# Attention and two feed-forward layers on one core: where the softmax probabilities of the later head pairs are divided by their sums

## The chip, the core and the metric

The kernel runs on one core of one Trainium2 chip. A core has five engines that run side by side, each with its own instruction queue worked off in order: TensorE (PE in the profile, its weight loads PEld), VectorE (DVE), ScalarE (ACT), GpSimd (POOL) and SyncE (SP), which here only issues DMAs. The metric is the device time of one execution in microseconds, the median of several runs.

## What is computed

```python
def _attn_ref(q, k, v, g_q, g_k):
    q_n, k_n = (rmsnorm(q, g_q), rmsnorm(k, g_k))
    scores = scale * np.matmul(q_n, k_n.transpose(0, 1, 3, 2))
    scores = scores - np.max(scores, axis=-1, keepdims=True)
    attn = np.exp(scores)
    attn = attn / (np.sum(attn, axis=-1, keepdims=True) + 1e-09)
    return np.matmul(attn, v)

x = attn_out.transpose(0, 2, 1, 3).reshape(B * S, H * D)
h = x @ w_in;  g = s * np.maximum(h, 0) ** 2 + b;  x = g @ w_out
h = x @ w2_in; g = h * np.cos(h);                  out = g @ w2_out
```

There are 4 batches of 12 heads, 448 positions and 64 values a head. The two feed-forward layers see 1792 rows of 768 values and are 2048 wide. Inputs of q, k, v are float32, the weights float64.

## The kernel before

**The work.** Two heads make a pair, so there are 24 pairs, six to a batch. A pair has four chunks of query rows: three of 128 rows, each for both heads, and a last one in which the 64 remaining rows of both heads share one tile. One step of the attention works on one chunk: `scores` multiplies q by k on TensorE (tile `sc`, in PSUM), VectorE finds the row maximum (`top`), and ScalarE takes the exponential into `pr` and adds up each row into `sums`. Two steps later `turn` transposes `pr` on TensorE in four pieces (tile `tp`) and VectorE and ScalarE copy the turned pieces to `pT`. When all four chunks of a pair are turned, `mix` multiplies `pT` by v on TensorE (tile `av`).

**The division.** The probabilities are not divided one by one. `reciprocals` lets GpSimd add 1e-9 to the seven columns of `sums`, VectorE takes reciprocals, and GpSimd spreads them over 64 columns each into `rb`. `spread` transposes `rb` on TensorE (four 128x128 pieces, tile `rt`, lines 354 to 361), so that the reciprocal of every query stands above its column, and ScalarE copies `rt` to `xf`. `finish` multiplies `av` by `xf` on VectorE. Then `keep` either splits the result into a high and a low half for the feed-forward layers (batches 0 and 1: `xha` on ScalarE, `xla` on GpSimd) or sends it to DRAM to be fetched back later (batches 2 and 3).

**The order of the work.** The first nine pairs (`ALONE = 9`) run nearly by themselves. From the tenth on, attention steps are woven between units of the first feed-forward layer: an "in" unit (tile `ph`, 18 matmuls of 448 columns, then ScalarE, GpSimd and VectorE make `gh` and `gl`) and an "out" unit (tile `po`, 6 matmuls, then VectorE adds it to `acc`, or ScalarE copies it there the first time). Every step returns a cost, a number that only paces the weaving. Weights are float64 and are taken apart by bit operations on VectorE (`c`, `t`), then split into `wh` on ScalarE and `wl` on GpSimd. The order in which each engine gets its instructions is settled when the program is built; at run time each engine takes them strictly in that order.

**Buffers that the steps speak of.** In the woven part `ph` and `po` take turns in two PSUM buffers (tag `mo`), so a unit can start when the unit two before it has been emptied. The score tiles, and from the tenth pair on also `pt`, `rt` and `av`, take turns in a ring of four PSUM buffers (tag `sc`, function `four`); a transposed chunk has two (`tp`). `pr` has six buffers in SBUF. `line("PE", ...)` chains all attention work on TensorE in one fixed order.

Of the kernel before, what the change touches and what calls it, by code (L numbers as in the profile page):

```python
# [10 lines left out]
F32 = mybir.dt.float32  # L11
# [4 lines left out]
ALU = mybir.AluOpType  # L16
# [17 lines left out]
def body(ctx, tc, q, k, v, g_q, g_k, w1_in, w1_out, s_in, b_in, w2_in, w2_out, out):  # L34
# [4 lines left out]
    P = 128  # L39
# [69 lines left out]
    def split(src, layer, b, eng=nc.gpsimd):  # L109
        done = xs.setdefault((layer, b), [])  # L110
        hi, lo = (z[:, b % 2 * S:(b % 2 + 1) * S] for z in home(layer, b)[len(done)])
        nc.scalar.copy(hi, src)  # L112
        eng.tensor_tensor(lo, src, hi.bitcast(F32), ALU.subtract)
        done.append(True)

# [18 lines left out]
    def attention(keep):  # L134
# [151 lines left out]
        def scores(s):  # L286
# [36 lines left out]
            exps.append(e)  # L323

# [9 lines left out]
        def turn(s):  # L334
            i, c = divmod(s, NCH)
            b, hp = pairs[i]
            if c == 0:
                for j in range(2):
                    st[i]["pT", j] = att.tile([CP, NCH, S], F32, tag=f"pT{j}", name=f"pT_{b}_{hp}_{j}")
            for z in range(2 if c < NW else 1):  # L340
# [5 lines left out]
                for j in ((z,) if c < NW else (0, 1)):  # L346
                    at, part = (slice(c * P, (c + 1) * P), src) if c < NW else (slice(CUT, S), src[:, :, j * HALF:(j + 1) * HALF])
                    dst = st[i]["pT", j][:, :, at]
                    if j:
                        line("DVE", nc.vector.tensor_copy(dst, part))  # L350
                    else:
                        line("ACT", nc.scalar.copy(dst, part))

        def spread(i):
            b, hp = pairs[i]
            rt = bank(i, (i, "r"), f"rt_{b}_{hp}")
# [4 lines left out]
            line("ACT", emptied((i, "r"), nc.scalar.copy(x[D:, CUT:], rt[D:, S:])))  # L361

        def mix(i, part):
# [4 lines left out]
            for kc in part:  # L368
                for j in range(2):
                    mm.append(nc.tensor.matmul(st[i]["pa"][j * D:(j + 1) * D, :], st[i]["v"][:, j, kc, :], st[i]["pT", j][:, kc, :], start=(kc == 0), stop=(kc == NCH - 1)))  # L370
# [4 lines left out]
        def finish(i):  # L375
            b, hp = pairs[i]
            x = st[i]["x"]
            line("DVE", emptied((i, "a"), nc.vector.tensor_tensor(x, st[i]["pa"], x, ALU.mult)))
            st[i].clear()
            if i < ALONE - 1:  # L380
                held.append((b, hp, x))
            else:
                keep(b, hp, x)
                finished["pairs"] += 1
# [30 lines left out]
        for s in range(n + 5):  # L415
# [10 lines left out]
            if r == 3 and old is not None and not alone:  # L426
                spread(old)
                mix(old, range(NCH))
                finish(old)
                cost += 3.86  # L430
# [11 lines left out]
            if r == 0:  # L442
                if 0 <= i - 2 < ALONE:
                    finish(i - 2)
                emit(reciprocals, i - 1)
# [381 lines left out]
```

## Time and profile before

| what | value |
|---|---|
| median of 3 runs | 1264.2 us (1260.06 to 1722.74) |
| profiled execution, its own time | 1266.07 us |
| its span in the profile | 1263.9 us |
| PE busy | 1235.9 us |
| DVE busy | 834.9 us |
| ACT busy | 745.0 us |
| POOL busy | 604.6 us |
| mean granted TensorE clock | 0.997 |

The span is the time from the first to the last recorded instruction; some 2 us of the execution's own time lie around it. Busy is the time in which an engine had at least one instruction in work. Matmuls overlap, so a matmul's own duration is longer than the distance from its start to the next one's; in this kernel the distances tell what a matmul costs.

### The profile page before, as it was taken

To read this page: it belongs to the slowest core of one execution; us is meant where nothing else is said; L and a number is where in the kernel's file an instruction comes from. 1 tells how busy PE (TensorE), PEld (TensorE's weight loads), DVE (VectorE), ACT (ScalarE), POOL (GpSimd) and SP (SyncE) were. 2 spreads that over 40 slices of the span, in tenths; PEclk is the share of its full clock that TensorE was granted. 3 is DMA by queue.
4 is the path that set the end of the run, shared out by engine and by line. 5 is a ranking of instruction groups with operands and counts; after the bars stand their busy time and mean duration, and the time that the engine had idled before them with its cause. 6 is when DMAs were issued, how large, how long until landed. Compare 5 with 4: busy or idle time off the path is not lost.

```text
span 1263.9 us, 18827 instructions
## 1 busy us (share of the span) xinstructions
PE 1235.9 (98%) x6629; PEld 1046.1 (83%) x6629; DVE 834.9 (66%) x1447; ACT 745.0 (59%) x1665; POOL 604.6 (48%) x724
## 2 busy tenths in 40 slices
PE   7999999999999999999999999999999999999998
PEld 5454677777786877889999999899999999999998
DVE  6777868868767674843444447765867766666755
ACT  5777888866665664435332225698665757566741
POOL 4666646555644425724332323555453535354531
PEclk9999999999999999999999999999999999999999
DMA  4233345534433333442221112121202111111105
GB/s 125 77 109 88 110 118 147 152 112 134 129 104 99 118 120 121 149 143 92 80 65 56 57 44 76 38 75 64 75 28 73 51 50 51 51 51 51 52 12 175
DMA packets 86734, 111.33 MB, mean 88 GB/s; under 512 B 11760, under 2 KB 76784, under 8 KB 86640
## 3 DMA queue, kind: packets, MB, share of 16 engines
q1 hardware_dynamic: 86320, 109.90, 28.5%
q8 instruction: 52, 0.85, 0.3%
q14 instruction: 42, 0.34, 0.1%
q10 hardware_dynamic: 320, 0.23, 0.1%
HBM read 86.51 MB, written 23.59 MB: 87 GB/s over the span
## 4 chain that ended last, share of the span: by engine, by line
PE 52%; ACT 2%; DVE 2%; POOL 1%; DMA 1%; issue 1%; POOLq 0%; SPq 0%; DVEq 0%; ACTq 0%
PE ph L547 25%; PE po L632 18%; PE po L606 9%; DMA raw<-in_moe_w_in_dram 1%; POOL wl L475 0%; DVE t L516 0%; ACT xha L112 0%; POOL gt L576 0%; ACT t L510 0%; DVE acc L614 0%; DVE gt L572 0%; ACT gh L577 0%; DVE t L517 0%; DVE c L515 0%; ACT wh L472 0%
## 5 line engine op out<-in xcount | busy, mean ns | idle before, releaser
L578 POOL TENSOR_TENSOR gl<-gt,gh 128x448 fp32r<-128x448 f32 (+2 forms) x128 | 152.0, 1194 | 165.0 <-ACT gh L577 164.9
L547 PE MATMUL ph<-xha,wh 128*128 128x448 f32 (+2 forms) x576 | 212.2, 370 | 1.3 <-DVE acc L614 0.8
L547 PE MATMUL ph<-xha,wl 128*128 128x448 f32 (+2 forms) x576 | 211.2, 367 | 0.0
L547 PE MATMUL ph<-xla,wh 128*128 128x448 f32 (+2 forms) x576 | 211.0, 367 | 0.0
L475 POOL TENSOR_TENSOR wl<-t,wh 128x384 fp32r<-128x384 f32 x128 | 139.9, 1109 | 97.5 <-ACT wh L472 93.0
L472 ACT CAST wh<-t 128x384 fp32r<-128x384 f32 x200 | 95.6, 512 | 114.8 <-PE po L606 48.7
L614 DVE TENSOR_TENSOR acc<-po,acc 128x448 f32<-128x448 f32 x168 | 102.5, 617 | 75.6 <-PE po L606 75.4
L632 PE MATMUL po<-wh,gh 128*128 128x384 f32 x448 | 151.5, 339 | 0.0
L632 PE MATMUL po<-wl,gh 128*128 128x384 f32 x448 | 150.1, 335 | 0.4 <-POOL wl L475 0.4
L632 PE MATMUL po<-wh,gl 128*128 128x384 f32 x448 | 150.2, 335 | 0.0
L606 PE MATMUL po<-gh,wh 128*128 128x448 f32 x384 | 144.8, 380 | 1.5 <-DVE acc L614 1.4
L640 DVE TENSOR_TENSOR acc<-po,acc 128x384 f32<-128x384 f32 x196 | 105.1, 550 | 60.0 <-PE po L632 59.9
L606 PE MATMUL po<-gh,wl 128*128 128x448 f32 x384 | 140.8, 367 | 0.0
L606 PE MATMUL po<-gl,wh 128*128 128x448 f32 x384 | 140.7, 367 | 0.0
L576 POOL TENSOR_TENSOR gt<-hs,gt 128x512 f32<-128x512 f32 x64 | 76.3, 1200 | 118.7 <-ACT gt L575 114.8
L321 ACT ACTIVATE pr<-sc,top 128x448 f32<-128x448 f32 x161 | 101.8, 638 | 43.6 <-DVE top L312 43.3
L516 DVE SCALAR_TENSOR_TENSOR t<-c,t 128x384 uint32<-128x384 uint32 x128 | 94.9, 745 | 42.2 <-ACT t L510 39.1
L561 POOL TENSOR_TENSOR r<-r 128x448 f32<-128x448 f32 x64 | 63.1, 986 | 120.6 <-ACT r L559 106.0
L547 PEld LDWEIGHTS ph<-xha,wh 128*128 128x128 f32 x576 | 108.2, 188 | 12.8 <-issue 1.2
L577 ACT CAST gh<-gt 128x448 fp32r<-128x448 f32 (+2 forms) x128 | 71.5, 566 | 80.0 <-DVE gt L563 48.4
L547 PEld LDWEIGHTS ph<-xla,wh 128*128 128x128 f32 x576 | 108.1, 188 | 10.9 <-issue 1.3
L547 PEld LDWEIGHTS ph<-xha,wl 128*128 128x128 f32 x576 | 108.2, 188 | 10.0 <-issue 0.6
(122 smaller groups left out, 2667.1 us busy)
## 6 DMA issues: line engine op xcount, KB each, us to landing
raw<-in_moe_w_in_dram SPq DMA_DIRECT2D x64, 384.0 KB, 3.5
raw<-in_moe_w_out_dram SPq DMA_DIRECT2D x64, 384.0 KB, 3.2
t<-wd SPq DMA_DIRECT2D x72, 192.0 KB, 2.4
wd<-t SPq DMA_DIRECT2D x64, 192.0 KB, 2.5
rawk<-in_k_dram SPq DMA_DIRECT2D x24, 224.0 KB, 2.9
rawv<-in_v_dram SPq DMA_DIRECT2D x24, 224.0 KB, 3.1
rawq<-in_q_dram SPq DMA_DIRECT2D x23, 192.0 KB, 3.2
xd<-xf SPq DMA_DIRECT2D x12, 224.0 KB, 2.8
```

The costliest lines, as they stand in the source:

```text
L321: e = line("ACT", nc.scalar.activation(pr, sc[j], AF.Exp, bias=tops[j], scale=scale[j], accum_out=st[i]["sums"][:, 2 * c + j:2 * c + j + 1]))
L472: z = nc.scalar.copy(wh, w)
L475: eng.tensor_tensor(wl, w, wh.bitcast(F32), ALU.subtract)
L516: nc.vector.scalar_tensor_tensor(t, c, 0x80000000, t, ALU.bitwise_and, ALU.bitwise_or)
L547: nc.tensor.matmul(h, a, m, start=(c == 0 and n == 0), stop=(c == NE - 1 and n == 2))
L576: nc.gpsimd.tensor_tensor(gt, h, gt, ALU.mult)
L577: nc.scalar.copy(gh, gt)
L578: nc.gpsimd.tensor_tensor(gl, gt, gh.bitcast(F32), ALU.subtract)
L606: marks["out"] = nc.tensor.matmul(po, a, m, start=(f == 0 and n == 0), stop=(f == CF - 1 and n == 2))
L614: nc.vector.tensor_tensor(at, po, at, ALU.add)
L632: nc.tensor.matmul(po, a, m, start=(f == 0 and n == 0), stop=(f == CF - 1 and n == 2))
L640: nc.vector.tensor_tensor(at, po, at, ALU.add)
```

## The change

From the tenth pair on (`i >= ALONE`) each chunk's probabilities are divided as soon as its row sums are there: GpSimd adds 1e-9, VectorE takes the reciprocal of the chunk's one or two columns, and GpSimd multiplies each `pr` tile in place by its column. What is turned is then already divided, and `spread` and the multiplication in `finish` are gone for these pairs: for batch 1 `finish` splits `av` straight out of PSUM (ScalarE and VectorE), for batches 2 and 3 ScalarE copies it to `xf`. For all pairs the turned probabilities of both heads stand in one tile, and the last chunk is copied there in one piece by ScalarE, where ScalarE and VectorE copied a half each. The step's cost falls from 3.86 to 3.38.

```diff
@@ scores
             exps.append(e)
+            if i >= ALONE:
+                part = st[i]["sums"][:, 2 * c:2 * c + len(tops)]
+                nc.gpsimd.tensor_scalar(part, part, 1e-9, 1.0, ALU.add, ALU.mult)
+                nc.vector.reciprocal(part, part)
+                for j in heads:
+                    pr = st[i]["pr", j, c]
+                    nc.gpsimd.tensor_scalar(pr, pr, part[:, j:j + 1], None, ALU.mult)
@@ turn
-                for j in ((z,) if c < NW else (0, 1)):
-                    at, part = (slice(c * P, (c + 1) * P), src) if c < NW else (slice(CUT, S), src[:, :, j * HALF:(j + 1) * HALF])
-                    dst = st[i]["pT", j][:, :, at]
-                    if j:
-                        line("DVE", nc.vector.tensor_copy(dst, part))
-                    else:
-                        line("ACT", nc.scalar.copy(dst, part))
+                if c == NW:
+                    line("ACT", nc.scalar.copy(pT[:, :, :, CUT:], tp.rearrange("p (k j q) -> p j k q", k=NCH, j=2)))
+                elif z:
+                    line("DVE", nc.vector.tensor_copy(pT[:, 1, :, c * P:(c + 1) * P], src))
+                else:
+                    line("ACT", nc.scalar.copy(pT[:, 0, :, c * P:(c + 1) * P], src))
@@ finish
+            if i >= ALONE:
+                pa = st[i]["pa"]
+                if b < 2:
+                    z = split(pa, 0, b, nc.vector)
+                else:
+                    x = att.tile([P, S], F32, tag="xf", name=f"xf_{b}_{hp}")
+                    z = nc.scalar.copy(x, pa)
+                    keep(b, hp, x)
+                emptied((i, "a"), z)
+                st[i].clear()
+                finished["pairs"] += 1
+                return
@@ the loop over steps
             if r == 3 and old is not None and not alone:
-                spread(old)
                 mix(old, range(NCH))
                 finish(old)
-                cost += 3.86
+                cost += 3.38
...
-                emit(reciprocals, i - 1)
+                if i <= ALONE:
+                    emit(reciprocals, i - 1)
```

What this does to the order of the instructions is shown at three places. A name such as `pr_2_1_2_0` is batch 2, pair 1 of the batch, chunk 2, head 0; `po_0_1_2_0` is layer 0, weight block 1, output block 2, batch 0.

TensorE at the end of the third pair of batch 2, before, with the four transposes of `rb` between the turned chunk and the product with v:

```order
L606 MATMUL po_0_1_5_0_3347<-gh_0_2_0_2680,wl_0_1_1_1_1_2895 128x448
L606 MATMUL po_0_1_5_0_3347<-gl_0_2_0_2681,wh_0_1_1_1_1_2894 128x448
L343 MATMUL tp_2_3_0_1_3329<-ident_76,pr_2_3_0_1_3147 112x128 x4
L357 MATMUL rt_2_2_3363<-ident_76,rb_105 128x128 x4
L370 MATMUL av_2_2_3371<-pT_2_2_0_2958,rawv_2_2_2862 64x448
L370 MATMUL av_2_2_3371<-pT_2_2_1_2959,rawv_2_2_2862 64x448
```

The same place now:

```order
L624 MATMUL po_0_2_4_0_3981<-gh_0_5_0_3426,wl_0_1_1_2_1_3541 128x448
L624 MATMUL po_0_2_4_0_3981<-gl_0_5_0_3427,wh_0_1_1_2_1_3540 128x448
L350 MATMUL tp_2_3_0_1_3249<-ident_76,pr_2_3_0_1_3090 112x128 x4
L376 MATMUL av_2_2_3339<-pT_2_2_2917,rawv_2_2_2829 64x448 x8
L298 MATMUL sc_2_3_3_0_3352<-kh_2_3_2913,qh_2_3_2854 128x448
```

The `rt` row is gone, and the pair stands beside a later unit of the feed-forward layer: weight block 2 instead of 1.

GpSimd after the second pair of batch 2, before, where one addition and three copies serve a whole pair:

```order
L229 TENSOR_TENSOR nk_2_4_2666<-rawk_2_4_2458,y_2_4_2833 112x2x4x64
L327 TENSOR_SCALAR sums_2_1_0_2514<-sums_2_1_0_2514 128x7
L329 COPY rb_105<-sums_2_1_0_2514 128x384
L332 COPY rb_105<-sums_2_1_0_2514 64x64 x2
L561 TENSOR_TENSOR r_0_4_1_3058<-r_0_4_1_3058 128x448
```

The same pair now, its third chunk alone (`wl` and `gl` are low halves of weights and of the feed-forward layer's activations):

```order
L326 TENSOR_SCALAR sums_2_1_0_2507<-sums_2_1_0_2507 128x2
L493 TENSOR_TENSOR wl_0_1_1_1_1_2935<-t_0_1_1_1_1_1_2952,wh_0_1_1_1_1_2934 128x384
L326 TENSOR_SCALAR sums_2_1_0_2507<-sums_2_1_0_2507 128x1
L596 TENSOR_TENSOR gl_0_4_0_3026<-gt_0_4_0_3030,gh_0_4_0_3025 128x448
L326 TENSOR_SCALAR sums_2_2_0_2772<-sums_2_2_0_2772 128x2
L493 TENSOR_TENSOR wl_0_1_0_5_0_3172<-t_0_1_0_5_0_0_3176,wh_0_1_0_5_0_3171 128x384
L596 TENSOR_TENSOR gl_0_4_0_3026<-gt_0_4_1_3056,gh_0_4_0_3025 128x448
L493 TENSOR_TENSOR wl_0_1_0_5_0_3172<-t_0_1_0_5_0_1_3189,wh_0_1_0_5_0_3171 128x384
L330 TENSOR_SCALAR pr_2_1_2_0_2630<-pr_2_1_2_0_2630,sums_2_1_0_2507 128x448
L330 TENSOR_SCALAR pr_2_1_2_1_2632<-pr_2_1_2_1_2632,sums_2_1_0_2507 128x448
```

Between the addition and the two multiplications of a chunk stand seven instructions, five of them 128x384 or 128x448 subtractions that other work needs.

VectorE between two additions of output units of batch 0, before, with attention work (`pT`, `top`, `kl`, `ss`) among the weights:

```order
L614 TENSOR_TENSOR acc_0_0_1_0_2283<-po_0_1_1_0_3081,acc_0_0_1_0_2283 128x448
L517 SCALAR_TENSOR_TENSOR t_0_1_0_6_0_1_3204<-c_0_1_0_6_0_1_3203,t_0_1_0_6_0_1_3204 128x384
L517 SCALAR_TENSOR_TENSOR t_0_1_1_2_0_0_3267<-c_0_1_1_2_0_0_3266,t_0_1_1_2_0_0_3267 128x384
L350 COPY pT_2_1_1_2651<-tp_2_1_3_0_2887 112x4x64
L282 SCALAR_TENSOR_TENSOR kl_2_3_2955<-pt_k_2_3_2935,gqk_84,kh_2_3_2954 128x448
L312 TENSOR_REDUCE top_2_2_0_2807<-sc_2_2_2_0_2940 128x1
L312 TENSOR_REDUCE top_2_2_0_2807<-sc_2_2_2_1_2941 128x1
L195 TENSOR_REDUCE ss_1_104<-nk_2_5_2974 112x8
L515 TENSOR_SCALAR c_0_1_1_2_0_1_3279<-c_0_1_1_2_0_1_3279 128x384
L515 TENSOR_SCALAR c_0_1_1_2_1_0_3514<-c_0_1_1_2_1_0_3514 128x384
L614 TENSOR_TENSOR acc_0_0_2_0_2369<-po_0_1_2_0_3125,acc_0_0_2_0_2369 128x448
```

The same units now, and the next:

```order
L632 TENSOR_TENSOR acc_0_0_1_0_2321<-po_0_1_1_0_3120,acc_0_0_1_0_2321 128x448
L533 TENSOR_SCALAR c_0_1_0_6_0_0_3263<-c_0_1_0_6_0_0_3263 128x384
L327 RECIPROCAL sums_2_1_0_2507<-sums_2_1_0_2507 128x2
L533 TENSOR_SCALAR c_0_1_0_6_0_1_3276<-c_0_1_0_6_0_1_3276 128x384
L327 RECIPROCAL sums_2_1_0_2507<-sums_2_1_0_2507 128x1
L632 TENSOR_TENSOR acc_0_0_2_0_2409<-po_0_1_2_0_3199,acc_0_0_2_0_2409 128x448
L534 SCALAR_TENSOR_TENSOR t_0_1_0_6_0_0_3264<-c_0_1_0_6_0_0_3263,t_0_1_0_6_0_0_3264 128x384
L327 RECIPROCAL sums_2_2_0_2772<-sums_2_2_0_2772 128x2
L535 SCALAR_TENSOR_TENSOR t_0_1_0_6_0_0_3264<-c_0_1_0_6_0_0_3263,t_0_1_0_6_0_0_3264 128x384
L632 TENSOR_TENSOR acc_0_0_3_0_2488<-po_0_1_3_0_3287,acc_0_0_3_0_2488 128x448
```

No score or turned chunk stands between these output units any more: on TensorE nine of them follow each other with no attention work among them.

## Rows read from the trace of the kernel before

**Rows 1.** The page, busy time of each engine over the whole span.

```profile
PE 1235.9 (98%) x6629; PEld 1046.1 (83%) x6629; DVE 834.9 (66%) x1447; ACT 745.0 (59%) x1665; POOL 604.6 (48%) x724
```

**Rows 2.** Windows, three stretches: length, busy time by engine, granted clock, DMA.

```profile
0.00:140.00 140.00, 123.98 (x723) 71.34 (x725) 104.46 (x207) 98.05 (x271) 84.75 (x168) 0.99 0.36 102
140.00:500.00 360.00, 355.94 (x2036) 275.77 (x2034) 265.17 (x481) 242.18 (x590) 190.80 (x270) 1.00 0.40 123
500.00:1263.90 763.90, 756.00 (x3874) 698.96 (x3870) 465.22 (x760) 404.79 (x806) 329.07 (x287) 1.00 0.23 69
```

**Rows 3.** Timeline of TensorE at one `spread`: start, duration, instruction.

```profile
304.39 0.36 PE L606 MATMUL po<-gl,wh 128*128 128x448 f32 x1
304.59 0.60 PE L343 MATMUL tp<-ident,pr 128*112 128x128 f32 x4
305.02 0.60 PE L357 MATMUL rt<-ident,rb 128*128 128x128 f32 x4
305.55 3.23 PE L370 MATMUL av<-pT,rawv 112*64 112x448 f32 x16
```

**Rows 4.** Groups by line and shape, GpSimd: busy us, mean ns, idle before.

```profile
L327 POOL TENSOR_SCALAR sums<-sums 128x7 f32<-128x7 f32 x24 | 5.3, 222 | 32.6 <-ACT pr L321 32.1
...
L329 POOL COPY rb<-sums 128x384 f32<-128x384 f32 x24 | 12.6, 527 | 5.6 <-DVE sums L328 4.3 <-PE sc L298 0.5 <-PE pt_q L254 0.4
...
L332 POOL COPY rb<-sums 64x64 f32<-64x64 f32 x48 | 12.3, 257 | 1.4
...
L578 POOL TENSOR_TENSOR gl<-gt,gh 128x448 fp32r<-128x448 f32 x64 | 75.8, 1185 | 83.8 <-ACT gh L577 83.6
```

**Rows 5.** Groups by line and shape, ScalarE and VectorE.

```profile
L360 ACT COPY xf<-rt 128x448 f32<-128x448 f32 x24 | 12.9, 538 | 0.0
...
L361 ACT COPY xf<-rt 64x64 f32<-64x64 f32 x24 | 5.0, 208 | 0.7
...
L352 ACT COPY pT<-tp 112x512 f32<-112x512 f32 x72 | 42.2, 586 | 26.3 <-PE tp L343 25.9
...
L378 DVE TENSOR_TENSOR xf<-av,xf 128x448 f32<-128x448 f32 x24 | 14.8, 615 | 13.2 <-PE av L370 13.2
...
L328 DVE RECIPROCAL sums<-sums 128x7 f32<-128x7 f32 x24 | 4.7, 195 | 7.5 <-POOL sums L327 7.4
```

**Rows 6.** Waits of TensorE from 140 to 505 us: total, times, longest.

```profile
PE sc L298 <- ACT pr L321: 3.6, 3, 2.0
```

**Rows 7.** Timeline of TensorE: eight transposes undisturbed, then behind a wait.

```profile
343.06 1.03 PE L343 MATMUL tp<-ident,pr 128*112 128x128 f32 x8
343.86 0.45 PE L606 MATMUL po<-gh,wh 128*128 128x448 f32 x1
...
390.67 0.47 PE L298 MATMUL sc<-kh,qh 64*128 64x448 f32 x2 [1.98 <-ACT pr L321]
...
391.49 1.53 PE L343 MATMUL tp<-ident,pr 128*112 128x128 f32 x8
```

**Rows 8.** Windows, the slice of that wait; columns as in rows 2.

```profile
380.00:400.00 20.00, 18.02 (x91) 12.15 (x89) 15.76 (x29) 11.63 (x29) 11.38 (x14) 0.91 0.37 117
```

**Rows 9.** Timeline of VectorE and GpSimd: one VectorE instruction, twice.

```profile
321.58 0.50 DVE L563 TENSOR_SCALAR gt<-r,sb 128x448 f32<-128x448 f32 x1
...
322.87 1.14 POOL L578 TENSOR_TENSOR gl<-gt,gh 128x448 fp32r<-128x448 f32 x1 [1.90 <-ACT gh L577]
...
324.97 2.14 POOL L475 TENSOR_TENSOR wl<-t,wh 128x384 fp32r<-128x384 f32 x2
...
325.04 1.19 DVE L563 TENSOR_SCALAR gt<-r,sb 128x448 f32<-128x448 f32 x1 [2.31 <-POOL r L561]
```

**Rows 10.** Timeline: an output unit's last matmul, and its addition on VectorE.

```profile
439.26 0.37 PE L606 MATMUL po<-gl,wh 128*128 128x448 f32 x1
...
440.24 1.18 DVE L563 TENSOR_SCALAR gt<-r,sb 128x448 f32<-128x448 f32 x1 [0.84 <-POOL r L561]
...
441.35 0.61 DVE L614 TENSOR_TENSOR acc<-po,acc 128x448 f32<-128x448 f32 x1
```

More of the change, by code (lines that the diff above doesn't have):

```diff
@@ L112, in split @@
         nc.scalar.copy(hi, src)
-        eng.tensor_tensor(lo, src, hi.bitcast(F32), ALU.subtract)
         done.append(True)
+        return eng.tensor_tensor(lo, src, hi.bitcast(F32), ALU.subtract)
     def wide(layer, seg, ck):
@@ L337, in turn @@
             if c == 0:
-                for j in range(2):
-                    st[i]["pT", j] = att.tile([CP, NCH, S], F32, tag=f"pT{j}", name=f"pT_{b}_{hp}_{j}")
+                st[i]["pT"] = att.tile([CP, 2, NCH, S], F32, tag="pT", name=f"pT_{b}_{hp}")
+            pT = st[i]["pT"]
             for z in range(2 if c < NW else 1):
@@ L345, in turn @@
                 src = tp.rearrange("p (k q) -> p k q", k=NCH)
-                for j in ((z,) if c < NW else (0, 1)):
-                    at, part = (slice(c * P, (c + 1) * P), src) if c < NW else (slice(CUT, S), src[:, :, j * HALF:(j + 1) * HALF])
-                    dst = st[i]["pT", j][:, :, at]
-                    if j:
-                        line("DVE", nc.vector.tensor_copy(dst, part))
-                    else:
-                        line("ACT", nc.scalar.copy(dst, part))
+                if c == NW:
[4 more added lines that the diff above has]
+                    line("ACT", nc.scalar.copy(pT[:, 0, :, c * P:(c + 1) * P], src))
         def spread(i):
             b, hp = pairs[i]
-            rt = bank(i, (i, "r"), f"rt_{b}_{hp}")
+            rt = psm.tile([P, 512], F32, tag="mo", name=f"rt_{b}_{hp}", bufs=2)
             mm = [nc.tensor.transpose(rt[:, c * P:(c + 1) * P], rb[:, c, :, :].rearrange("p h d -> p (h d)"), ident) for c in range(NW + 1)]
@@ L360, in spread @@
             line("ACT", nc.scalar.copy(x, rt[:, :S]))
-            line("ACT", emptied((i, "r"), nc.scalar.copy(x[D:, CUT:], rt[D:, S:])))
+            line("ACT", nc.scalar.copy(x[D:, CUT:], rt[D:, S:]))
         def mix(i, part):
@@ L369, in mix @@
                 for j in range(2):
-                    mm.append(nc.tensor.matmul(st[i]["pa"][j * D:(j + 1) * D, :], st[i]["v"][:, j, kc, :], st[i]["pT", j][:, kc, :], start=(kc == 0), stop=(kc == NCH - 1)))
+                    mm.append(nc.tensor.matmul(st[i]["pa"][j * D:(j + 1) * D, :], st[i]["v"][:, j, kc, :], st[i]["pT"][:, j, kc, :], start=(kc == 0), stop=(kc == NCH - 1)))
             line("PE", mm[0], mm[-1])
@@ L376, in finish @@
             b, hp = pairs[i]
+            if i >= ALONE:
[10 more added lines that the diff above has]
+                return
             x = st[i]["x"]
-            line("DVE", emptied((i, "a"), nc.vector.tensor_tensor(x, st[i]["pa"], x, ALU.mult)))
+            line("DVE", nc.vector.tensor_tensor(x, st[i]["pa"], x, ALU.mult))
             st[i].clear()
```

## The prediction

> **What bounds the kernel now.** I read the busy times of the page first: TensorE has work in 1235.9 of 1263.9 us, no other engine in more than 834.9 [rows 1]. So time is won by taking work from TensorE, and lost where it is made to wait. Then the windows, cut where the stages change: up to 140 us the first nine pairs, from 140 to 500 the woven part, in which nearly all that the change touches lies, and from 500 on the feed-forward layers alone [rows 2]. In the woven part TensorE is busy 355.94 of 360 us; VectorE 265.17 (74%), ScalarE 242.18, GpSimd 190.80 (53%). Last the waits of TensorE there: three waits of scores for an exponential, 3.6 us together, one of them 1.98 us long [rows 6, 7]. So the saving is a count of TensorE's instructions, and the risk lies in what VectorE and GpSimd, now hidden behind it, are given.
>
> **What leaves TensorE.** Fifteen pairs lose their four `rt` transposes. In the timeline the transposes of a chunk start at 304.59, those of `rt` at 305.02, the product with v at 305.55 [rows 3]. With `rt` gone the product starts between 0.43 us (what four transposes before it take) and 0.53 us (the whole distance) earlier: 15 x 0.43 = 6.5 to 15 x 0.53 = 8.0 us. I take 7.2. TensorE has no slack in this stage, so all of it shows unless a wait takes it back.
>
> **What leaves the PSUM ring.** `rt` took one of the ring's four buffers in turn; without it a pair asks for ten instead of eleven, and scores find a free buffer sooner. What this can give is the three waits, 3.6 us, and what followed the longest: after 1.98 us of waiting eight transposes took 1.53 us instead of 1.03, and the slice shows a granted clock of 0.91 [rows 7, 8], a stretch at the lower level, 1.2 GHz, before TensorE was back at 2.4; 0.09 x 20 us = 1.8 us. Together 5.4 us at most, 0 if other tiles cause them. I take half, 2.7.
>
> **ScalarE and VectorE.** ScalarE loses 15 copies of 0.538 and 15 of 0.208 us (11.2), gains 12 copies of `av` for batches 2 and 3 (by the first of these rows 6.5), and 15 half copies of the last chunk become whole ones (at most 0.586 each, 8.8): at most 4.1 us more in 360, hidden, as 118 us are idle. VectorE loses 15 multiplications (0.615, 9.2) and 15 half copies, gains 45 reciprocals (0.195, 8.8) and three subtractions of batch 1 that leave GpSimd: about even [rows 5]. What would hurt is not their sum but where a reciprocal stands in a queue; that is below.
>
> **GpSimd.** Per pair it loses 0.222 + 0.527 + 2 x 0.257 = 1.26 us and gains four additions (0.222) and seven multiplications of 448 columns [rows 4]. The trace has no such multiplication. The copy of 384 columns takes 0.527, the addition on 7 columns 0.222: 0.305 / 377 = 0.81 ns a column, so 0.58 us for 448. The bounds are 0.222 (all fixed cost) and 1.185 (the subtraction of two such tiles). The copy has one input as the multiplication has, so I take 0.58. 105 x 0.58 + 60 x 0.222 - 15 x 1.26 = 55 us more (18 to 119): GpSimd goes from 190.8 to 246 us in 360, 68% (58 to 86). It stays below TensorE, but a chunk's transposes now wait for it, and in order.
>
> **What the new waits cost.** First, the transposes. In the new order four of the 105 transposed tiles stand only 10 to 13 matmuls (0.20 us each [rows 3], so 2.1 to 2.7 us) behind work that GpSimd must have seen before it reaches their multiplication; the others have 4 us and more. The short chain is the matmul's end 0.37, one ScalarE copy 0.54, one GpSimd subtraction 1.19, the multiplication 0.58: 2.7 us with no queue. Up to 1 us late each, I take 3 us for the four; 0 if queues are empty, and the upper end is the second rival. Behind a late transposed tile the whole chain of attention work on TensorE stands, and the feed-forward matmuls behind that in the queue.
>
> Second, the output units. Since attention work is held up until GpSimd has multiplied, the new order has stretches of output units in a row. 25 feed-forward units on TensorE now begin with 0.4 to 1.7 us of matmuls, mostly 1.2, since the unit that used their PSUM buffer; before, none had under 2. Their waits: from the last matmul's start to the end of its addition were 441.35 + 0.61 - 439.26 = 2.70 us where VectorE was busy with something else [rows 10], 0.37 + 0.61 = 0.98 us where it is free. The next user of the buffer wants it 0.20 + 1.22 = 1.42 us after that start. So each costs 0 to 1.28 us, 0 to 32 in all. VectorE is free a quarter of the time, seven of the units wait for ScalarE instead, and in these stretches VectorE has no attention work to do; I take 0.15 each, 4 us.
>
> Third, at the attention's end the last product with v and one input unit stand right behind what they need; about one copy of 0.586 us and its queue each, 1.5 us (0 to 3).
>
> **The sum.** Profiled execution 1266.1 - 7.2 - 2.7 + 3 + 4 + 1.5 = 1264.7. That execution was 1.9 us above the median of the runs shown, so the median should be 1262.8, say 1263 us: a little is won on TensorE and most of it given back in waits. Its own range, with half of each wait either way, is 1257 to 1270.
>
> **Rival one: the clean gain.** GpSimd keeps ahead, additions find VectorE free, and both gains come whole: 1264.2 - 7.2 - 5.4 = 1251.6, 1252 us. For it: GpSimd has 47% of the woven part idle, and most multiplications have 5 to 15 us until their transposes. Against it: the 25 tight units are in the order whatever GpSimd does.
>
> **Rival two: TensorE stops for the multiplications.** Place: the first transposes of a chunk in the woven part. A stop of the size seen costs the wait, 2.0 us, and the stretch at the lower clock behind it, 1.8: 3.8 us [rows 7, 8]. From two stops on the gain is eaten; over 2% slower (25 us) needs (25.3 + 7.2) / 3.8 = 8.6, nine stops. With one in every second pair: 1264.2 - 7.2 + 7.5 x 3.8 = 1285 us. For it: additions, reciprocals and multiplications of a chunk are strung through two queues with up to seven foreign instructions between them, and twelve of the tiles have under 6.2 us. Against it: a stop gives GpSimd time to catch up, and two steps lie between a chunk's scores and its transposes.
>
> **Rival three: VectorE is held up by GpSimd.** The same VectorE instruction took 0.50 us with GpSimd idle and 1.19 us while GpSimd ran [rows 9]. 105 more GpSimd instructions can stretch as many on VectorE, 105 x 0.58 = 61 us, which would take it from 265 to 326 of 360 us (91%). Then additions come late for the tight units: half of 1.28 us for 25 of them, 1264.2 - 7.2 + 25 x 0.64 = 1273 us. Against it: the additions read PSUM, and the one in rows 10 took 0.61 us with GpSimd at work.
>
> The Trainium skill, SBUF - State Buffer, "Who interferes with whom", says that VectorE and GpSimd share a port pair that one instruction holds exclusively while the other blocks fully, and that it concerns VectorE instructions in a two-port mode or with two SBUF inputs. Rows 9 agree for the first kind (0.50 against 1.19 us). By that rule the 61 us above would be lost on VectorE whole; by the rows a stretched instruction costs nothing while TensorE has other work, and that is what I go by.
>
> **How the numbers follow.** Forecast 0.52, clean gain 0.22, stops for the multiplications 0.14, VectorE held up 0.12. The range takes in the clean gain and the second rival's middle case: 1252 to 1285. Two per cent, about what a measurement of this kernel can tell from no change, is 25 us. No case gains as much (the clean gain ends 12.6 us below the median): 0.02. Slower by more takes nine stops, half of the second rival, or the third with more than the half price: 0.09. The rest, 0.89, is within.
>
> **What would show it.** Right: no `rt` in the woven part, TensorE's busy time there shorter by some 7 us; GpSimd's multiplications near 0.58 us and its share at two thirds; TensorE's waits led by output units for `acc`, 4 us or so, and by transposes for GpSimd, 3 us. Wrong: multiplications at 1 us or more; transposes waiting in most pairs, with slices of the woven part below a clock of 1.00 (rival two); the VectorE groups `gt`, `t` and `c` with means up by half (rival three); or no wait on TensorE at all (rival one).

## The result, and the profile after

The changed kernel takes 1271.92 us (median of 6 runs, 1266.79 to 1275.34), the kernel before it beside it 1266.16 us (6 runs): a ratio of 1.0063, 95% interval 1.0042 to 1.0084. Two of the six runs of the kernel before were slow (1722.74 and 2013.07 us), and the ratio, taken from the fast runs alone, is not that of the medians. It is slower by 8 us (0.0063 x 1266), where 1 us of gain was forecast. The profiled execution took 1268.42 us, with a span of 1266.6 us.

The page, busy time of each engine, answering to [rows 1]:

```profile
PE 1227.9 (97%) x6569; PEld 1042.7 (82%) x6569; DVE 838.1 (66%) x1456; ACT 744.0 (59%) x1647; POOL 754.7 (60%) x826
```

TensorE has 60 instructions less and is busy 8.0 us less, and yet the span is 2.7 us longer: its idle time is 1266.6 - 1227.9 = 38.7 us, where it was 28.0. Windows of the changed kernel, the stretches of [rows 2] and the 20 us in which the first divided pair begins; columns are length, busy time of TensorE, weight loads, VectorE, ScalarE, GpSimd, then granted clock, DMA share and GB/s:

```profile
0.00:140.00 140.00, 122.33 (x704) 68.82 (x704) 106.78 (x200) 97.87 (x267) 89.28 (x174) 0.97 0.37 105
140.00:500.00 360.00, 347.46 (x1954) 268.73 (x1951) 262.77 (x490) 239.67 (x572) 330.73 (x361) 0.99 0.38 118
500.00:1266.60 766.60, 758.14 (x3916) 705.11 (x3914) 468.55 (x766) 406.49 (x808) 334.70 (x293) 1.00 0.23 71
125.00:145.00 20.00, 15.97 (x87) 8.74 (x87) 13.44 (x28) 12.74 (x35) 16.86 (x28) 0.83 0.33 103
```

The same 20 us of the kernel before:

```profile
125.00:145.00 20.00, 19.46 (x126) 12.59 (x126) 17.55 (x34) 17.01 (x47) 12.11 (x27) 1.00 0.46 131
```

In the woven part TensorE is busy 347.46 us, 8.5 less than before, and GpSimd 330.73 (92%) instead of 190.80. At the beginning of the divided pairs 3.5 us of TensorE's work are missing, and the granted clock is 0.83: part of the stretch ran at the lower level, 1.2 GHz. Groups by line and shape, GpSimd, answering to [rows 4]:

```profile
L330 POOL TENSOR_SCALAR pr<-pr,sums 128x448 f32<-128x448 f32 x105 | 162.1, 1553 | 9.4 <-DVE sums L327 8.5
...
L326 POOL TENSOR_SCALAR sums<-sums 128x2 f32<-128x2 f32 x45 | 10.8, 241 | 6.9 <-ACT pr L321 3.2
```

A multiplication takes 1.55 us in the mean, not 0.58. Waits of TensorE from 140 to 505 us (total, times, longest), answering to [rows 6]:

```profile
PE po L624 <- DVE acc L632: 7.3, 5, 3.0
PE tp L350 <- POOL pr L330: 1.9, 1, 1.9
PE po L624 <- ACT acc L630: 1.6, 1, 1.6
PE po L624 <- ACT r L577: 0.8, 1, 0.8
```

The output units wait for their additions, as foreseen, and one transpose for GpSimd. The longest wait lies ahead of this stretch. The timelines of GpSimd and of TensorE there (start, duration, instruction, in brackets the wait before it):

```profile
130.99 0.19 POOL L326 TENSOR_SCALAR sums<-sums 128x2 f32<-128x2 f32 x1 [0.72 <-ACT pr L321]
...
131.57 1.20 POOL L229 TENSOR_TENSOR nq<-rawq,y 128x384 f32<-128x384 f32 x2
132.72 1.05 POOL L229 TENSOR_TENSOR nk<-rawk,y 112x512 f32<-112x512 f32 x1
133.74 2.81 POOL L330 TENSOR_SCALAR pr<-pr,sums 128x448 f32<-128x448 f32 x2
...
131.47 0.37 PE L298 MATMUL sc<-kl,qh 64*128 64x448 f32 x2
135.21 1.10 PE L350 MATMUL tp<-ident,pr 128*112 128x128 f32 x4 [3.37 <-POOL pr L330]
136.60 1.10 PE L350 MATMUL tp<-ident,pr 128*112 128x128 f32 x4 [0.29 <-POOL pr L330]
```

The first two multiplications stand behind a later pair's norms (`nq`, `nk`) in GpSimd's queue, and these behind the addition of a chunk's 1e-9, which waited 0.72 us for its exponential. TensorE stands 3.37 us for the first multiplication. The four transposes behind it take 1.10 us, where eight took 1.03 [rows 7]: half speed.

### The profile page after: what moved, and what is told of

The parts are those of the page before. It is cut to its first block, busy times and chain, and to the rows that moved or that the text cites. A ratio compares the mean times of both kernels' runs of the same rounds, so it can differ in the third digit from the quotient of the medians.

```text
span 1266.6 us, 18890 instructions
## 1 busy us (share of the span) xinstructions
PE 1227.9 (97%) x6569; PEld 1042.7 (82%) x6569; DVE 838.1 (66%) x1456; ACT 744.0 (59%) x1647; POOL 754.7 (60%) x826
## 4 chain that ended last, share of the span: by engine, by line
PE 72%; DVE 5%; ACT 2%; POOL 2%; issue 1%; DMA 1%; ACTq 0%; DVEq 0%; POOLq 0%
PE ph L565 33%; PE po L650 18%; PE po L624 15%; PE av L376 2%; PE tp L350 2%; PE sc L298 2%; DVE t L534 1%; DVE t L535 1%; DVE acc L632 1%; DVE top L312 1%; POOL pr L330 0%; POOL wl L493 0%; DVE gt L581 0%; DVE c L533 0%; ACT t L528 0%
## 5 line engine op out<-in xcount | busy, mean ns | idle before, releaser
L330 POOL TENSOR_SCALAR pr<-pr,sums 128x448 f32<-128x448 f32 x105 | 162.1, 1553 | 9.4 <-DVE sums L327 8.5
L534 DVE SCALAR_TENSOR_TENSOR t<-c,t 128x384 uint32<-128x384 uint32 x128 | 99.3, 779 | 37.1 <-ACT t L528 33.6
L312 DVE TENSOR_REDUCE top<-sc 128x1 f32<-128x448 f32 x168 | 98.3, 616 | 36.4 <-PE sc L298 35.6
```

The source lines that it names most:

```text
L312: line("DVE", nc.vector.tensor_reduce(tops[j], sc[j], axis=AX.X, op=ALU.max, negate=True))
L330: nc.gpsimd.tensor_scalar(pr, pr, part[:, j:j + 1], None, ALU.mult)
L534: nc.vector.scalar_tensor_tensor(t, c, 0x80000000, t, ALU.bitwise_and, ALU.bitwise_or)
```

## The experiments

Two theories stood against each other. Load: 105 long instructions fill GpSimd, which then delays the subtractions of the feed-forward layer. Wait: a chunk's transposes reach TensorE before its multiplied tiles, which stand behind other work in a queue, whatever they cost. Ratios are to the kernel before, run beside each; 0.001 is 1.27 us. All but the run of prices (one execution) were timed in five rounds.

**Left out.** The multiplications are gone, all else stays.

> The changed kernel with the 105 multiplications on GpSimd left out (the later pairs' probabilities are not divided at all). Theory A, the price: a multiplication takes 1.4 us or more on GpSimd instead of the 0.58 I took, GpSimd is full in the woven part, and what comes late behind it costs TensorE; then this kernel is faster than the kernel before by the transposes saved, ratio 0.990 to 0.996, and its program has no tight output units. Rival B, the other parts: the loss comes from the 45 more reciprocals, the one-piece copies or the split out of PSUM; then the ratio stays at 1.003 to 1.008.

Measured 0.9887 (0.9864 to 0.991), 1251.27 us: 14 us under the kernel before, 22 under the changed one (by the ratios), and more than the 0.990 to 0.996 expected. In the woven part TensorE is busy 356.02 us, GpSimd 179.07:

```profile
140.00:500.00 360.00, 356.02 (x2008) 276.94 (x2007) 262.88 (x500) 241.96 (x577) 179.07 (x263) 1.00 0.41 126
```

So all that is lost hangs on the multiplications.

**One part alone.** The kernel before with only the merged tile and the last chunk's one copy:

```diff
-                for j in range(2):
-                    st[i]["pT", j] = att.tile([CP, NCH, S], F32, tag=f"pT{j}", name=f"pT_{b}_{hp}_{j}")
+                st[i]["pT"] = att.tile([CP, 2, NCH, S], F32, tag="pT", name=f"pT_{b}_{hp}")
...
+                if c == NW:
+                    line("ACT", nc.scalar.copy(pT[:, :, :, CUT:], tp.rearrange("p (k j q) -> p j k q", k=NCH, j=2)))
```

> The kernel before with one part of the change alone: both heads' turned probabilities in one tile and the last chunk copied in one piece, the division as before. My account of the gain without the multiplications (about 14 us by the run that left them out) gives it all to the spread and its transposes, so this should be a ratio of 0.998 to 1.002. The rival is that the one copy in place of two, and the freer ScalarE and VectorE, carry a part of the 14 us: then 0.993 to 0.997.

Measured 0.9969 (0.9957 to 0.9981): the merged tile gives 4 of the 14 us, if the parts add. My account was wrong here, and the rival's figure came.

**The load alone.** The kernel before, with 105 multiplications of constants on GpSimd whose result nobody reads:

```diff
+            if i >= ALONE:
+                for j in heads:
+                    idle = att.tile([P, 4, S // 4], mybir.dt.bfloat16, tag="idle", name=f"idle_{key}_{j}", bufs=1)
+                    follow(nc.gpsimd.tensor_scalar(idle, ident[:, :S // 4].unsqueeze(1).to_broadcast([P, 4, S // 4]), halfpi, None, ALU.mult), e)
```

> The kernel before with 105 multiplications of 448 columns more on GpSimd, each behind the exponential it would belong to, of a constant into a scratch tile that nobody reads: the load without the wait. Theory A as a matter of load: about 1.4 us each, GpSimd to about 340 of 360 us, weights and low halves late, ratio 1.004 to 1.015. Rival C, the wait: the transposes wait for nothing new, ratio 0.999 to 1.003.

Measured 1.009 (1.0066 to 1.0114), 11 us: work that nobody waits for costs time too. It is not quite the load of the change, though. Its multiplications take the same (1.40 us in the median), but VectorE is busy 282.07 us of the woven part here, where it is 265.17 in the kernel before and 262.77 in the changed one. So a part of the 11 us may come over VectorE in a way that the change does not.

**The wait almost without the load.** The changed kernel, each multiplication on 4 columns:

```diff
-                    nc.gpsimd.tensor_scalar(pr, pr, part[:, j:j + 1], None, ALU.mult)
+                    nc.gpsimd.tensor_scalar(pr[:, ::CP], pr[:, ::CP], part[:, j:j + 1], None, ALU.mult)
```

> The changed kernel with each GpSimd multiplication done on 4 of its 448 columns only: most of the division is left out, so the output isn't the reference's, but every wait between the exponentials, GpSimd and the transposes stays. Theory A (the GpSimd engine's time in the woven part is what costs, 105 instructions at 1.4 to 1.55 us): with some 0.1 to 0.2 us each the load is gone and the time is that of the kernel without the multiplications plus a little, a ratio of 0.988 to 0.992 to the kernel before. Theory B (the wait itself costs, the longer way from an exponential to its transposes over another engine): the time stays well above, 0.997 to 1.006. In between, both have a share.

Measured 0.994 (0.9918 to 0.9961), between the two theories: at a median of 0.30 us a multiplication, 7 us of the 14 are gone. Both have a share.

**Other engines.** The same line on VectorE (`nc.vector.tensor_scalar`), on ScalarE (`nc.scalar.activation(pr, pr, AF.Copy, scale=part[:, j:j + 1])`), on ScalarE without the line that adds 1e-9, on GpSimd as a product of two tensors (`nc.gpsimd.tensor_tensor(pr, pr, part[:, j:j + 1].to_broadcast([P, S]), ALU.mult)`), and the first head on ScalarE, the second as such a product.

> The multiplications on VectorE in place of GpSimd. Theory A: 0.35 to 0.5 us each by the nearest rows (0.34 for 384 columns of c, 0.50 for 448 of gt), VectorE from 265 to about 310 of 360 us, TensorE keeps most of the saving, ratio 0.992 to 1.000. If the wait of the transposes for a division of any engine is what costs (rival C, the added wait): as the changed kernel, 1.003 to 1.008.

> The multiplications on ScalarE. Theory A: 0.55 to 0.6 us each, ScalarE from 242 to about 300 of 360 us, ratio 0.992 to 1.000. Rival C, the added wait: 1.003 to 1.008.

> The multiplications on ScalarE and the addition of 1e-9 left out for the later pairs (a sum is at least 1, so the addition changes no float32 value), so that VectorE's reciprocal waits for ScalarE alone. If the length of the chain from exponential to transposes still costs, below the 0.9976 of the multiplications on ScalarE: 0.992 to 0.996. If only ScalarE's load costs: 0.996 to 0.999.

> The changed kernel with the multiplication on GpSimd written as a product of two tensors, the second the column repeated over 448 columns. Theory A, price and load: about 1.0 us each by the row of nk and nq, GpSimd to about 290 of 360 us instead of 331, ratio to the kernel before 0.994 to 1.001. Rival C, the wait for GpSimd at any price: 1.004 to 1.008.

> Head 0's multiplications on ScalarE, head 1's on GpSimd as a product of two tensors. Theory A: ScalarE 242 + 60 x 0.6 = 278, GpSimd 172 + 45 x 1.0 + 13 = 230 of 360 us, no engine beside TensorE over 80%, ratio 0.990 to 0.996, as fast as the multiplications left out or nearly. If sharing only adds waits: 0.997 to 1.003.

| where | ratio | 95% interval | one of 105, us |
|---|---|---|---|
| VectorE | 1.0055 | 1.0037 to 1.0073 | 0.45 |
| ScalarE | 0.9976 | 0.9959 to 0.9994 | 0.67 |
| ScalarE, no addition | 0.996 | 0.9946 to 0.9975 | 0.67 |
| GpSimd, two tensors | 1.0126 | 1.0105 to 1.0148 | 0.94 |
| ScalarE and GpSimd | 0.9984 | 0.9969 to 1.0 | 0.67 and 0.93 |

(Medians.) Without the addition ScalarE's ratio is 0.0016 lower, 2 us, but the intervals overlap, so this pair doesn't settle what the addition costs. On VectorE the ratio is what the added wait would give, on ScalarE what the price would. VectorE is then busy 302.26 of the 360 us, and from 100 to 505 us TensorE's scores wait for exponentials nine times, 7.7 us. The product of two tensors is the slowest of all, outside what either theory expected, though it is cheaper than what the change does. So price alone doesn't decide. VectorE's groups in the woven part show what else it does; with the product of two tensors:

```profile
L534 DVE SCALAR_TENSOR_TENSOR t<-c,t 128x384 uint32<-128x384 uint32 x51 | 47.6, 938 | 15.9 <-ACT t L528 14.6 <-ACT ln L204 0.3
L535 DVE SCALAR_TENSOR_TENSOR t<-c,t 128x384 uint32<-128x384 uint32 x51 | 43.2, 850 | 0.7
```

and with the change as it was made:

```profile
L534 DVE SCALAR_TENSOR_TENSOR t<-c,t 128x384 uint32<-128x384 uint32 x52 | 36.3, 702 | 5.6 <-ACT t L528 4.8
L535 DVE SCALAR_TENSOR_TENSOR t<-c,t 128x384 uint32<-128x384 uint32 x52 | 39.2, 759 | 0.5
```

VectorE's instructions with two inputs are stretched by the product (938 and 850 ns against 702 and 759), far less by the multiplication by a column. That this stretching is what makes the product slow was not tested.

**Prices.** On GpSimd, idle at the end of the kernel before, three of each kind.

> The kernel before with GpSimd instructions put behind its last addition, when every engine is idle, three of each kind on 448 columns of a scratch tile: a multiplication by a column, the same on half the columns, by a constant, by a constant with an addition, by a column read as a second tensor, of a tensor by itself, a copy; then one by a column on ScalarE and on VectorE. If the form (a column as scalar operand) is what is dear: 1.4 us, half of it on half the columns, by a constant 0.6 or so, as a second tensor 1.0. If 1.4 is what the woven part's contention makes of it: 0.6 here. The time of this run says nothing.

Timeline of GpSimd (start, duration of the three together):

```profile
1259.73 4.40 POOL L804 TENSOR_SCALAR probe_x<-probe_x,halfpi 128x448 f32<-128x448 f32 x3
1264.23 2.71 POOL L806 TENSOR_SCALAR probe_x<-probe_x,halfpi 128x224 f32<-128x224 f32 x3
1267.03 4.15 POOL L808 TENSOR_SCALAR probe_x<-probe_x 128x448 f32<-128x448 f32 x3
1271.26 1.86 POOL L810 TENSOR_SCALAR probe_x<-probe_x 128x448 f32<-128x448 f32 x3
1273.20 2.95 POOL L812 TENSOR_TENSOR probe_x<-probe_x,halfpi 128x448 f32<-128x448 f32 x3
...
1279.25 1.80 POOL L816 COPY probe_y<-probe_x 128x448 f32<-128x448 f32 x3
```

L804 multiplies by a column (4.40 / 3 = 1.47 us), L808 by a constant (1.38), L810 multiplies by a constant and adds one (0.62), L812 is the product of two tensors (0.98), L816 a copy (0.60). The form with one operation takes over twice as long as the form with two; of the 1.47 us the column accounts for 0.09.

**The price that the prediction took.** So a second operation that changes nothing should bring the multiplication near 0.58 us:

```diff
-                    nc.gpsimd.tensor_scalar(pr, pr, part[:, j:j + 1], None, ALU.mult)
+                    nc.gpsimd.tensor_scalar(pr, pr, part[:, j:j + 1], 1.0, ALU.mult, ALU.mult)
```

> The changed kernel with the GpSimd multiplication written with two operations, times the column and then times 1.0, the result being the same. In the run of prices the form with two operations took 0.62 us for 448 columns where the form with one took 1.4. Theory A (the price of the multiplication is what failed in the prediction, 0.58 us foreseen, 1.4 to 1.55 found): at 0.6 to 0.7 us GpSimd falls from 92% to about 70% of the woven part and the time to 0.990 to 0.996 of the kernel before. Theory B (the wait over GpSimd, or its traffic beside VectorE, costs at any price): no better than 0.999 to 1.006, as the product of two tensors was at 1.03 us. Should the column operand be what makes it slow and not the single operation, it takes 1.4 us again and the time is that of the changed kernel, 1.004 to 1.008.

One line's instructions (minimum, median, maximum in ns), and the window:

```profile
L330 POOL TENSOR_SCALAR pr<-pr,sums x105: 634/642/2396, 134.1 to 479.9; 128x448 f32<-128x448 f32 x105
```

```profile
140.00:500.00 360.00, 349.71 (x1958) 266.18 (x1956) 264.08 (x491) 239.68 (x571) 249.53 (x358) 1.00 0.39 119
```

The price is 0.64 us and GpSimd at 249.53 us in the woven part (69%; the prediction had 246), and still the ratio is 1.0025 (1.0013 to 1.0037). The price took back 1.0063 - 1.0025 = 0.0038, 5 us, and left 17 of the 22.

**Begun later.** Dividing on GpSimd from the twelfth pair on (`i >= ALONE + 2`), two more pairs by the spread.

> The changed kernel, but divided on GpSimd only from the twelfth pair on; the tenth and eleventh keep the spread of the reciprocals. Theory C (a third to a half of the loss arises where the multiplication begins, at the tenth pair, where TensorE has nothing else to fill the wait of 3.4 us with and then runs at half clock for a stretch): the wait is gone from there, and the ratio falls by about 0.005, to 0.999 to 1.002, though three spreads of reciprocals and some rt transposes come back. Theory A (GpSimd's load through the whole woven part): about a ninth less load there, ratio 1.003 to 1.006.

Measured 1.0004 (0.999 to 1.0019), the figure of theory C, but not quite by its mechanism: the wait at the beginning is not gone, it moved along and became smaller. (The profiled execution, 1268.18 us, is the slowest of the eleven, so its waits may be larger than usual.) Window and TensorE's timeline 30 us later, where the kernel before is busy throughout:

```profile
160.00:180.00 20.00, 17.25 (x90) 10.95 (x88) 12.75 (x25) 13.79 (x36) 18.49 (x23) 0.83 0.30 90
```

```profile
163.86 0.47 PE L299 MATMUL sc<-kh,qh 64*128 64x448 f32 x2 [1.61 <-ACT pr L322]
...
165.08 0.65 PE L351 MATMUL tp<-ident,pr 128*112 128x128 f32 x4 [0.34 <-POOL pr L331]
166.47 1.10 PE L351 MATMUL tp<-ident,pr 128*112 128x128 f32 x4 [0.74 <-POOL pr L331]
```

TensorE waits once for an exponential and twice for the multiplication, and again the clock falls to 0.83 in the slice.

**A step later.** The decisive runs turn each chunk from the tenth pair on three steps behind its scores and ahead of the next ones, instead of two steps behind and after them. No instruction is added, and GpSimd's load stays.

```diff
+            late = s - 3
+            if NCH * ALONE <= late < n:
+                turn(late)
+                cost += 0.9 if late % NCH < NW else 0.45
             if s < n:
                 scores(s)
...
-            if LAG_T <= s < n + LAG_T:
-                turn(s - LAG_T)
-                cost += 0.9 if (s - LAG_T) % NCH < NW else 0.45
+            late = s - LAG_T
+            if 0 <= late < min(n, NCH * ALONE):
+                turn(late)
+                cost += 0.9 if late % NCH < NW else 0.45
```

It was put on the changed kernel, on the form with two operations, on that form without the additions of 1e-9 (left out of the divided pairs' sums, which are at least 1, since the row maximum is taken off before the exponential), on ScalarE without additions, on both engines (first head ScalarE, second GpSimd with two operations, no additions), and, as a control, on the kernel without multiplications.

> The changed kernel, with the chunks of the tenth pair and on turned three steps behind their scores and ahead of the next scores, instead of two steps behind and after them; everything else, GpSimd's load too, is the same. Theory D (what costs is that the transposes reach TensorE before the multiplied tiles, which stand behind other work in GpSimd's queue): the wait of 3.4 us at the tenth pair and the later ones go, the ratio falls from 1.006 to 0.996 to 1.001. Theory A (the load on GpSimd, which holds up the weights' and the gate's subtractions and so VectorE's sums): 1.003 to 1.008.

> The same step later for the transposes, with the GpSimd multiplication in its form with two operations (0.64 us). Theory D: with neither the price nor the wait, most of the gain of the kernel without multiplications shows, a ratio of 0.990 to 0.996. Theory A, or an effect of GpSimd's work on the other engines at any price: 1.000 to 1.004, as with two operations alone.

> The same step later, with the multiplication on ScalarE and without the additions of 1e-9 ahead of the reciprocals (this stays off GpSimd; the sums are at least 1, so the result is the reference's within its tolerance). Theory D: from 0.996 without the later step to 0.990 to 0.993, the fastest so far that computes all. If the wait on the way over ScalarE was small already: 0.995 to 0.998.

> The kernel without the multiplications (they are left out, the output isn't the reference's), with the chunks turned the same step later. It is the control of the three runs before it. Theory D (the later step helps because it covers the multiplication): here it has nothing to cover, so the ratio stays at 0.987 to 0.991, as without it (0.9887). Rival (the later step is a better order by itself, whatever is multiplied): 0.979 to 0.985, the same 0.4 to 0.8% lower.

> The multiplication on GpSimd with two operations, the chunks turned a step later, and the additions of 1e-9 left out (the sums are at least 1). The additions are 60 instructions of 0.25 us on GpSimd and one step of the way from the sums to the multiplication. Theory D: a shorter way still helps a little, 0.991 to 0.994 where with them it is 0.9947; if the step later already covers all, 0.994 to 0.996.

> First head's probabilities multiplied on ScalarE, second head's on GpSimd with two operations, no additions, chunks turned a step later. If what is left of the loss is the load on whichever engine takes all 105 multiplications, half on each comes closer to the kernel without them: 0.989 to 0.991, below the 0.9919 with ScalarE alone. If each added engine only adds a wait, 0.992 to 0.995.

| kernel | as it was | a step later | interval of the latter |
|---|---|---|---|
| the change | 1.0063 | 0.9981 | 0.9969 to 0.9993 |
| two operations | 1.0025 | 0.9947 | 0.9933 to 0.996 |
| two operations, no additions | not run | 0.9908 | 0.9884 to 0.9931 |
| ScalarE, no additions | 0.996 | 0.9919 | 0.9906 to 0.9932 |
| both engines, no additions | not run | 0.9895 | 0.9874 to 0.9916 |
| without multiplications | 0.9887 | 0.9882 | 0.986 to 0.9904 |

The step takes 10 us off the change and off its cheaper form, 5 off the one on ScalarE, and nothing off the control. So its gain hangs on the multiplication, and it isn't a better order by itself. How it works is less simple than theory D says. In the first of them GpSimd is as busy as in the changed kernel (330.87 against 330.73 us), and its multiplications take the same (1.41 us in the median of either). The woven part and two stretches of 20 us, TensorE's waits from 140 to 505 us, and its timeline at the first divided chunk:

```profile
140.00:500.00 360.00, 348.86 (x1967) 268.94 (x1965) 267.43 (x491) 240.40 (x574) 330.87 (x368) 0.99 0.39 120
125.00:145.00 20.00, 17.17 (x110) 10.69 (x109) 15.59 (x32) 15.66 (x43) 16.67 (x26) 1.00 0.39 117
160.00:180.00 20.00, 16.07 (x78) 11.35 (x80) 13.08 (x27) 13.82 (x35) 19.33 (x24) 0.83 0.23 71
```

```profile
PE tp L350 <- POOL pr L330: 6.0, 4, 1.9
PE po L629 <- DVE acc L637: 4.6, 5, 2.2
PE po L629 <- ACT acc L635: 0.3, 1, 0.3
```

```profile
135.48 0.65 PE L350 MATMUL tp<-ident,pr 128*112 128x128 f32 x4 [1.71 <-POOL pr L330]
136.87 0.65 PE L350 MATMUL tp<-ident,pr 128*112 128x128 f32 x4 [0.74 <-POOL pr L330]
```

The first stop is 1.71 us where it was 3.37, and the clock stays at 1.00 around it. But other stops have come: from 140 us on TensorE waits 6.0 us for multiplications where it waited 1.9, and from 100 us on 8.5 us in six waits, none above 1.9, where the changed kernel has 5.5 in three. What fell is the waits of output units, 4.6 us for VectorE after 7.3, and the share of the lower clock: in slices of 20 us from 100 to 500 us the changed kernel shows 0.86, 0.97, 0.91 and 0.91 and otherwise 1.00, this one a single 0.83. In all TensorE idles 34.1 us instead of 38.7 and is busy 1225.4 instead of 1227.9, with as many instructions. So theory D's figure came, but not its mechanism: at 1.41 us a multiplication the step makes the longest stop shorter and does not do away with the waiting. With two operations it comes closer: from 100 us on TensorE waits 2.2 us for multiplications with the step, 4.3 without it.

With two operations and no additions (this profiled execution, 1247.86 us, is the fastest of six whose median is 1252.94), the window, TensorE's waits from 140 to 505 us, and its timeline at the first divided chunk:

```profile
140.00:500.00 360.00, 353.98 (x2010) 275.24 (x2010) 269.67 (x496) 241.37 (x578) 246.03 (x307) 1.00 0.41 125
```

```profile
PE sc L298 <- ACT pr L321: 2.6, 4, 1.3
PE po L628 <- DVE acc L636: 2.5, 2, 2.3
PE tp L349 <- POOL nq L229: 0.6, 1, 0.6
```

```profile
130.62 1.72 PE L375 MATMUL av<-pT,rawv 112*64 112x448 f32 x8
132.36 1.27 PE L349 MATMUL tp<-ident,pr 128*112 128x128 f32 x8
```

The transposes follow at once where TensorE stood 3.37 us, by the step, the price and the missing additions together, and the list of TensorE's waits names no multiplication any more. The fastest two that still divide: on both engines 1251.56 us (0.9895) and on GpSimd alone 1252.94 us (0.9908), the kernel before standing at 1265.0 beside them. Their intervals overlap, and with that of the control.

## Why the prediction was wrong, point by point

The sum gave 3 + 4 + 1.5 = 8.5 us to all that the divisions on GpSimd would cost, and they cost 22.

**What leaves TensorE and the ring: right as a sum.** Without multiplications the gain is 14.3 us (0.0113 x 1265). Of that 3.9 (0.0031 x 1265) come from the merged tile; 10.4 are left if the two add, against 7.2 + 2.7 = 9.9 forecast. No run tells the two terms apart.

**ScalarE and VectorE: the size failed.** I put their loads at "about even, hidden". They are even (239.67 and 262.77 us against 242.18 and 265.17 [rows 2]), but the merged tile alone gives 3.9 us. Which of its two edits, the tile or the copy, does so wasn't tried.

**GpSimd: the price failed, beyond its bounds.** I took 0.58 us "by the copy", within 0.222 to 1.185; it takes 1.41 (median) to 1.55 (mean). The copy does cost 0.60 and the addition was rightly read: both are of kinds that are fast here. What the trace of before didn't show is that a `tensor_scalar` with one operation is a slower kind, since every `tensor_scalar` that GpSimd runs in that kernel, the addition of [rows 4] among them, has two. The price carries 5 us (change against two operations), and 4.3 with the step later (0.9981 - 0.9947).

The Trainium skill, GPSIMD Engine Reference, "4.1 Engine selection", says that elementwise work with one input runs on GpSimd at roughly line rate. The copy (0.60 us for 448 columns) and the form with two operations (0.62) don't speak against it; the form with one operation took 1.38 to 1.47 us, and there the measurement decides.

**What the new waits cost, first, the transposes: this step failed most.** I counted four tiles of 105 that are tight in the order and put "3 us for the four". They cost more. In the trace of the changed kernel the transposes wait 5.5 us for multiplications, in three waits, and the stretch at the lower clock comes on top. The step later, which moves nothing but the place of the transposes, gives back 10 us at either price (0.0082 and 0.0078), part of it, by the traces, in the waits of output units and in the clock. Two things were missed. Distance in the order is no time where there is nothing to fill it: at the tenth pair no feed-forward unit stands between the scores and these transposes, so TensorE reaches them at once, whereas the multiplication stands behind 2.2 us of norms (131.57 to 133.74). And a stop has a second part: of the 20 us around the first one 3.5 us of work are missing and the clock is 0.83, up to another 0.17 x 20 = 3.4 us. That is rival two's mechanism (3.8 us a stop), to which I gave 0.14; it came with a few stops, not with one in every second pair.

**The load itself: costed at nothing.** "It stays below TensorE" was no cover. With the step later and the price at 0.64 us, leaving out the additions still gives 5 us (0.9947 to 0.9908), though they are 60 instructions of 0.24 us; they lie on the way to the multiplication as well as on GpSimd, and hold up what stands behind them in its queue (the norms behind the one at 130.99). Which of these counts isn't settled. From there to the control 3 us are left (0.9908 to 0.9882), within the intervals; but the control still has the additions, and one without them was not run. The account of the 22 us, by steps: price 5, step later 10, additions 5, rest 3 (23, as it ends at the control with the step, 0.9882). The steps after the price were measured one upon the other, so another order would split them a little differently. That load on GpSimd without any wait for it costs time is shown by the run with the load alone (11 us). How it reaches TensorE there isn't settled: in the profiled execution, the fastest of the six, TensorE idles 5.7 us more than in the kernel before, and one wait of an output unit for its addition is 4.9 us long.

**Second, output units: right in kind, sized low.** TensorE's waits in the woven part are led by them, 7.3 us for VectorE's additions and 1.6 for ScalarE's copies, where I took 4 (0 to 32). **Third, the attention's end** (1.5 us) could not be told apart.

**Rival three** (VectorE held up by GpSimd) did not happen as priced: VectorE's busy time in the woven part went down by 2.4 us, not up by 61, though `t` rose from 685 and 630 ns to 702 and 759 and `c` from 450 to 516, while `gt` fell from 760 to 723. The rows of before for `t`, in the woven part:

```profile
L516 DVE SCALAR_TENSOR_TENSOR t<-c,t 128x384 uint32<-128x384 uint32 x53 | 35.8, 685 | 14.2 <-ACT t L510 13.7
L517 DVE SCALAR_TENSOR_TENSOR t<-c,t 128x384 uint32<-128x384 uint32 x53 | 33.1, 630 | 0.6
```

The rule weighed there, of the Trainium skill, SBUF - State Buffer, "Who interferes with whom", is that a VectorE instruction with two SBUF inputs contends with a GpSimd one that reads SBUF. Beside the product of two tensors the rows agree (938 and 850 ns); beside the multiplication of the change, which reads SBUF as well, the rise is a few per cent in one group and a fifth in the other.

**Rival one**, the clean gain at 1252 us, is what the change gives once the step and the two-operation form are there and the additions gone (1252.94), with GpSimd at 246.03 us in the woven part, the 246 that the prediction had computed. The number was right for a kernel that this one was not, and by luck: the clean gain leaves out the 3.9 us of the merged tile, and the 246 counts the additions that this kernel has not.

## What to carry to other kernels

When work is put between a producer and the engine that sets the time, count the queue ahead of it on the new engine, and ask what the bound engine has to do meanwhile at that very place, at the beginning above all; a later turn of the consumer may cost no instruction and give back much (10 of 22 us here). Price an instruction by a row of the same form (number of operations, number of inputs), not only of the same shape; if there is no such row, a probe at an idle end tells it in one run. And an engine with time to spare isn't free: cheaper multiplications on GpSimd, busy 92% of the woven part, were worth 5 us here, and fewer additions, at about 70%, another 5.

## What was not expected of the hardware

On GpSimd, 448 columns times a scalar took 1.38 to 1.47 us with one operation, 0.62 with two. Half the columns took 0.90 (2.71 / 3), so (4.40 - 2.71) / 3 = 0.56 us hang on 224 columns, 2.5 ns each, where the form with two operations takes at most 0.62 / 448 = 1.4 ns. Why the form with less to do takes longer stays open. A product of two tensors on GpSimd, 0.94 us, slowed the kernel more than the one-operation form at 1.4 us, with one of VectorE's two-input instructions stretched by over a third (938 against 685 ns). And on VectorE itself, at 0.45 us the cheapest place for the multiplication, the kernel was no faster than with it on GpSimd (1.0055 against 1.0063).
